# Keys, values and phi loaded as five tokens on partitions 0 to 63 and four on 64 to 127, with constant products from the first phi on

## The chip, the cores and the metric

The kernel runs on one core of a Trainium2 chip. The metric is the device time of one launch in microseconds (us). Three runs of the kernel before gave a median of 747.67 us (747.43 to 747.82). One more execution was taken by the profiler, and all rows below come from that one.

## What is computed

An attention with a memory of 32 slots per head, followed by a two-layer network with a squared ReLU:

```python
a = exp(phi - max(phi, axis=seq)); a = a / (sum(a, axis=seq) + 1e-9)    # phi: 8, 8, 576, 32
k_m = einsum("bhsm,bhsd->bhmd", a, k)                                    # q, k, v: 8, 8, 576, 64
v_m = einsum("bhsm,bhsd->bhmd", a, v)
attn = softmax(q @ k_m.T / 8)                                            # 576 x 32 per head
x = (attn @ v_m) as 4608 rows of 512
h = relu(x @ w_in)                                                       # 512 x 2048, float64
out = (h * h) @ w_out                                                    # 2048 x 512, float64
```

Sums over the sequence take tokens in any order, as long as phi, k and v have the same one.

## The kernel before

Everything is in float32, and the large products are made of pairs of reduced-precision parts (a high part `gh`, `ath`, `wi[.,0]` and a low part `glo`, `atl`, `wi[.,1]`), three products each. `w_in` and `w_out` come as float64 and are decoded on the chip (`decode`, L486): one 512 KB piece is loaded as `raw` (L501), taken apart by four VectorE instructions and one of ScalarE (L503 to L507), copied and subtracted (L516 to L528), and `w_in` is written back to a scratch in DRAM (`w_in_kept`, L530) for later rounds (`wi_again`, L534).

One unit of `memory(b, hh)` (L575) handles four heads of one batch: it loads phi, k and v, takes the largest phi (`fold` L568, `pmx` products L599 and L602, L601), subtracts it (L603), takes the exponential (L605), and forms sums (`pkv`, L633) and the products with k and v (`pkv`, `pkw`, L621). For the first two batches the products are scaled (L657, L658), turned (L656) and kept as `kbd` and as `VT` high and low (`values`, L712, L713, its high part by the helper of L418). There are 16 units. `attention(b)` (L969) loads q, forms scores (`psc`), a softmax (L960 to L966) and `ath`, `atl` (L945, L946); `mm1` and `mm2` (L1005, L1039) are the two layers for one slice of 128 of the 2048 hidden columns and one batch: `h` products at L1024, accumulations at L1055, L1056 and L1058. The last three batches take another path with fewer products (`fast`, L1136).

The tokens of a unit lie on the partitions as `tokens` (L543) puts them: 512 tokens as four on each of the 128 partitions, and the other 64 as a fifth on partitions 0 to 63, with two DMAs for each tensor. Partitions 64 to 127 have no fifth token; phi is filled with -3e38 there (L580). The products run over the five columns, the fifth with 64 partitions.

The order of all instructions is fixed by a planner when the program is built. Every operation is recorded with a cost for each engine that may do it, a set of things it reads and writes, and sometimes a due time. `order` (L169) makes keys from the latest possible start of each operation, adds 100 ns times an entry of the table `MOVED` by the operation's task number, and places the operations on the engines in a run through the plan (`forward`, L225); that order is then written out. DMAs are costed by their bytes and a rate by the size of one piece (`rate`, L420), and most are issued on SP's queue, in plan order; SP's queue waits at an instruction until its buffer is free, so all that stands behind it waits too. `filled` (L195) then walks over PE's operations and puts constant products (`filler`, L433: `minus` times `minus`, 128x512, into a PSUM bank that is free) into planned gaps. A gap is filled only between the planned times of `FILL`, from 18,000 ns on before; each product is taken for 230 ns, and before `WARM` (20,500 ns) only one product is written into a gap.

Of the kernel before, what the change touches and what calls it, by code (L numbers as in the profile page):

```python
# [19 lines left out]
P = 128  # L20
# [344 lines left out]
def tile_attention_moe(  # L365
# [177 lines left out]
    def tokens(d, dst, src):  # L543

        d(dst[:, :, 0:NMAIN], src[:, 0:SM].rearrange("h (p c) d -> p h c d", c=NMAIN))
        d(dst[0:LEFT, :, NMAIN], src[:, SM:S].rearrange("h p d -> p h d"))
# [942 lines left out]
```

## Time and profile before

| | before |
|---|---|
| median of 3 runs | 747.67 us |
| profiled execution | 747.32 us |
| its span | 745.6 us |
| instructions | 16009 |
| busy: PE / VectorE / ScalarE / GpSimd | 726.2 / 581.7 / 430.0 / 62.2 us |
| DMA packets, bytes | 82158, 136.22 MB |

The span runs from the first to the last instruction; the execution's own time has 1.7 us more around it. Busy time is the time that an engine's instructions cover. PE's rows are modelled at their ends, so a busy PE says that it did not wait, not that it ran at its best rate.

### The profile page before, as it was taken

Reading aid. Unit: us, or ns where it says so; the run is one execution under the profiler, and the core shown is the slowest. Engines: PE = TensorE matmul, PEld = TensorE weight load, DVE = VectorE, ACT = ScalarE, POOL = GpSimd, SP = SyncE. Lnnn points to the kernel's source line nnn. Section 1 sums busy time; section 2 is a strip of 40 time slices with the busy share of each in tenths; the row PEclk is TensorE's granted clock in tenths of the full one; section 3 lists DMA queues with packets and bytes.
Section 4 is the critical chain, followed back from the end, with each engine's and each line's share of the span. In section 5 each row is a group of like instructions: output and inputs, shape, how many; then the busy total and the mean of one; then the engine's idle time right before and its main releaser. Section 6 shows DMA issues by size and latency. Waiting matters only on the chain.

```text
span 745.6 us, 16009 instructions
## 1 busy us (share of the span) xinstructions
PE 726.2 (97%) x5879; PEld 640.0 (86%) x5879; DVE 581.7 (78%) x1513; ACT 430.0 (58%) x991; POOL 62.2 (8%) x119
## 2 busy tenths in 40 slices
PE   5999999999999999999999999999999999999997
PEld 4778888888878887888888788888999999999997
DVE  3899989975579779966554674999799768997984
ACT  2687789765553454644444433767477455665651
POOL 4100001000100100002121220001000010000000
PEclk9999999999999999999999999999999999999999
DMA  8988876674566756554899679103674255445521
GB/s 246 321 289 286 253 252 211 226 218 130 156 183 209 207 170 165 159 151 118 314 335 359 178 231 270 36 1 75 184 195 136 71 153 150 134 126 150 151 67 43
DMA packets 82158, 136.22 MB, mean 183 GB/s; under 512 B 26368, under 2 KB 52992, under 8 KB 82080
## 3 DMA queue, kind: packets, MB, share of 16 engines
q1 hardware_dynamic: 68704, 102.59, 47.5%
q0 software_dynamic: 13280, 32.48, 13.0%
q8 instruction: 47, 0.77, 0.4%
q14 instruction: 31, 0.25, 0.1%
q10 hardware_dynamic: 96, 0.13, 0.1%
HBM read 100.34 MB, written 34.80 MB: 181 GB/s over the span
## 4 chain that ended last, share of the span: by engine, by line
PE 80%; DVE 9%; DMA 6%; SPq 2%; issue 1%; ACT 1%; DVEq 0%; ACTq 0%
PE h L1024 14%; PE h L1162 10%; PE acc L1058 8%; PE acc L1055 8%; PE acc L1056 8%; PE accl L1274 3%; PE accl L1290 3%; PE pkv L621 3%; PE pvw L756 2%; DMA raw<-in_moe_w_out_dram 2%; PE pvq_pv L789 2%; DMA vw<-vw_kept 2%; PE psc L850 2%; PE Mb L1222 1%; PE Mb L1219 1%; PE Mc L1222 1%
## 5 line engine op out<-in xcount | busy, mean ns | idle before, releaser
L1024 PE MATMUL h<-ath,vw 128*128 128x256 f32 (+1 forms) x640 | 130.8, 301 | 0.0
L1055 PE MATMUL acc<-wo,gh 128*128 128x512 f32 x320 | 127.7, 399 | 0.0
L1056 PE MATMUL acc<-wo,gh 128*128 128x512 f32 x320 | 125.8, 393 | 0.0
L1024 PEld LDWEIGHTS h<-ath,vw 128*128 128x128 f32 x640 | 103.1, 189 | 9.7 <-issue 0.9
L1058 PE MATMUL acc<-wo,glo 128*128 128x512 f32 x320 | 110.1, 402 | 0.2 <-DVE glo L1034 0.2
L1162 PE MATMUL h<-ath,vw 128*128 128x256 f32 (+1 forms) x384 | 78.5, 297 | 2.8 <-DMA vw<-vw_kept 1.5
L1030 ACT ACTIVATE gh<-r 128x512 fp32r<-128x512 f32 x80 | 50.5, 633 | 50.9 <-PE acc L1056 42.6
L1034 DVE TENSOR_TENSOR glo<-r,gh 128x512 fp32r<-128x512 f32 x80 | 54.7, 686 | 23.1 <-PE acc L1058 12.3
L1058 PEld LDWEIGHTS acc<-wo,glo 128*128 128x128 f32 x320 | 58.8, 188 | 14.6 <-issue 1.3
L1055 PEld LDWEIGHTS acc<-wo,gh 128*128 128x128 f32 x320 | 60.3, 189 | 10.9 <-issue 0.8
L1056 PEld LDWEIGHTS acc<-wo,gh 128*128 128x128 f32 x320 | 60.3, 188 | 10.8
L1024 PE MATMUL h<-atl,vw 128*128 128x320 f32 (+1 forms) x320 | 68.7, 296 | 0.1
L1028 ACT ACTIVATE r<-h 128x320 f32<-128x320 f32 (+1 forms) x120 | 47.6, 408 | 28.4 <-PE h L1024 20.4
L1162 PEld LDWEIGHTS h<-ath,vw 128*128 128x128 f32 x384 | 59.6, 189 | 4.4 <-issue 2.4
L418 ACT CAST vw<-pvw 64x512 fp32r<-64x512 f32 (+1 forms) x64 | 37.2, 582 | 27.0 <-PE pvw L756 19.7
L1024 PEld LDWEIGHTS h<-atl,vw 128*128 128x128 f32 x320 | 51.4, 189 | 0.5 <-DVE atl L946 0.3
L1032 ACT ACTIVATE r<-r 128x576 f32<-128x576 f32 x68 | 46.5, 684 | 1.1
L1190 ACT CAST H<-X 128x512 fp32r<-128x512 f32 x48 | 29.7, 618 | 21.4 <-DVE X L1183 10.5
L1191 DVE TENSOR_TENSOR LA<-X,H 128x512 fp32r<-128x512 f32 x48 | 33.1, 690 | 10.3 <-ACT H L1190 9.4
L1162 PE MATMUL h<-atl,vw 128*128 128x256 f32 (+1 forms) x192 | 41.0, 295 | 0.0
L764 DVE TENSOR_TENSOR vw<-pvw,vw 64x512 fp32r<-64x512 f32 x48 | 33.0, 687 | 7.6 <-ACT vw L418 6.6
L1162 PEld LDWEIGHTS h<-atl,vw 128*128 128x128 f32 x192 | 30.8, 189 | 0.0
(238 smaller groups left out, 1745.9 us busy)
## 6 DMA issues: line engine op xcount, KB each, us to landing
vw<-vw_kept SPq DMA_DIRECT2D x224, 128.0 KB, 3.9
wi<-w_in_kept SPq DMA_DIRECT2D x40, 512.0 KB, 5.4
vw_kept<-fold POOLq DMA_DIRECT2D x32, 512.0 KB, 6.1
KV<-in_k_dram SPq DMA_DIRECT2D x16, 512.0 KB, 4.7
KV<-in_v_dram SPq DMA_DIRECT2D x16, 512.0 KB, 5.8
raw<-in_moe_w_out_dram SPq DMA_DIRECT2D x16, 512.0 KB, 4.6
raw<-in_moe_w_in_dram SPq DMA_DIRECT2D x16, 512.0 KB, 7.2
w_in_kept<-wi POOLq DMA_DIRECT2D x16, 512.0 KB, 4.4
```

The source lines that it names most:

```text
L418: nc.scalar.copy(o, i) if e == "ACT" else ENG[e].tensor_copy(o, i)
L764: vec({"DVE": 700}, lambda e, part=part, pr=pr: nc.vector.tensor_sub(part(1), pw()[pr], part(0).bitcast(F32)), [pw, (V, (0, hf))], [(V, (1 ...
L1024: nc.tensor.matmul(p()[:, 0:n], V()[:, l, hh, c0:c0 + P], x()[:, hh, cs], start=(i == 0), stop=(i == 5))
L1028: op({"ACT": act(n) - 40, **({} if b < 2 else {"DVE": tt(n)})}, lambda e, cs=cs, n=n, p=p: nc.scalar.activation(r()[:, cs], p()[:, 0:n], A ...
L1030: op({"ACT": act(SM)}, lambda e: nc.scalar.activation(gh(), r()[:, 0:SM], AF.Square), [r], [gh])
L1032: op({"ACT": act(S), **({} if b < 2 or b == FAST - 1 else {"DVE": tt(S)})}, lambda e: nc.scalar.activation(r(), r(), AF.Square) if e == "A ...
L1034: vec({"DVE": tt(SM)}, lambda e: nc.vector.tensor_sub(glo(), r()[:, 0:SM], gh().bitcast(F32)), [r, gh], [glo])
L1055: nc.tensor.matmul(a(), gh()[:, c], t()[:, 0], start=f0, stop=False)
L1056: nc.tensor.matmul(a(), gh()[:, c], t()[:, 1], start=False, stop=False)
L1058: nc.tensor.matmul(a(), glo()[:, c], t()[:, 0], start=False, stop=f1)
L1162: nc.tensor.matmul(p()[:, at:at + n], V()[:, l, hh, f0:f0 + P], x()[:, hh, cs], start=(i == 0), stop=(i == 5))
L1191: vec({"DVE": tt(w * P)}, lambda e, x=x, hi=hi, lo=lo: nc.vector.tensor_sub(lo().rearrange("p o f -> p (o f)"), x(), f32(hi())), src + [(H ...
```

## The change

The 576 tokens of a head are cut differently: 320 go as five to each of the partitions 0 to 63, and 256 as four to each of the partitions 64 to 127. Each tensor still takes two DMAs, now one for each half of the partitions. The computation on them stays as it was, since the fifth column still has 64 partitions. The planner's table of rates gets entries for the two new piece sizes. `FILL` starts at 2,600 ns, a product planned before `WARM` is taken for 460 ns, and a gap gets as many as fit, before `WARM` too. The table `MOVED` is another one, so that the order of most of the program is new.

```diff
--- before.py
+++ after.py
@@ -29,34 +29,33 @@
 LEAD = 9000
 PART = 12
 MOVED = {
-    3: -480, 10: -3, 11: -6, 12: -1857, 13: -293, 22: 16, 24: -61, 26: -179, 28: 907, 30: 489, 32: -418, 34: 108,
...
+    1: -1373, 2: -1775, 3: 343, 6: 5, 7: 2, 12: -569, 13: -129, 22: 34, 26: -1498, 28: 153, 38: -1375, 46: 1173,
...
 }
 SEES = {"DVE": 125, "ACT": 150, "PE": 200, "POOL": 60, "SP": 0}
 MARGIN = 250
 BANKS = "acc", "h", "pv", "pa"
-FILL = 18000, 90000
+FILL = 2600, 90000
 FREE = "h.0", "h.1", "pa.0", "pv.0", "acc.3", "acc.2", "acc.1", "acc.0"
 COLD, WARM = 1.8, 20500
 OPENS, SLOW, RAMP = 1950.0, 1.2, 7500
@@ -201,12 +200,13 @@
         holds, t, full = {}, FILL[0], []
         for o in out:
             if o.left == "PE":
-                n = int((o.start - t - 590) / 230)
+                each = 230 if t > WARM else 460
+                n = int((o.start - t - 590) / each)
                 idle = [x for x in FREE if x not in holds or (not left[holds[x][0]] and holds[x][1] + 300 < t)]
                 if n > 0 and idle and FILL[0] <= t < FILL[1]:
                     f = Op()
-                    f.ways, f.left, f.start, f.end = {"PE": 90 + 230 * n}, "PE", t, t + 90 + 230 * n
-                    f.fn, f.deps, f.users, f.lead = self.filler(idle[-1], n if t > WARM else 1), set(), [], True
+                    f.ways, f.left, f.start, f.end = {"PE": 90 + each * n}, "PE", t, t + 90 + each * n
+                    f.fn, f.deps, f.users, f.lead = self.filler(idle[-1], n), set(), [], True
                     full.append(f)
                 t = o.start + o.ways["PE"]
             for b in o.uses:
@@ -417,7 +417,7 @@
     def copy(e, o, i):
         nc.scalar.copy(o, i) if e == "ACT" else ENG[e].tensor_copy(o, i)
 
-    rate = {128: 100, 256: 220, 512: 288, 1024: 300, 2048: 312, 4096: 325, 4608: 190}
+    rate = {128: 100, 256: 220, 512: 288, 640: 292, 1024: 300, 1280: 303, 2048: 312, 4096: 325, 4608: 190}
 
     def dma(fn, parts, r=(), w=(), eng="SP", issue=520, **more):
 
@@ -542,8 +542,8 @@
 
     def tokens(d, dst, src):
 
-        d(dst[:, :, 0:NMAIN], src[:, 0:SM].rearrange("h (p c) d -> p h c d", c=NMAIN))
-        d(dst[0:LEFT, :, NMAIN], src[:, SM:S].rearrange("h p d -> p h d"))
+        d(dst[0:LEFT], src[:, 0:SC * LEFT].rearrange("h (p c) d -> p h c d", c=SC))
+        d(dst[LEFT:P, :, 0:NMAIN], src[:, SC * LEFT:S].rearrange("h (p c) d -> p h c d", c=NMAIN))
 
     def vt_alloc(n):
         for i in (0, 1) if n == 0 else (1 - n % 2,):
@@ -578,7 +578,7 @@
         A = st([P, 4 * SC * M], F32, "phi", f"phi{u}", 2)
         a = lambda: A().rearrange("p (h c m) -> p h c m", h=4, c=SC)
         op({"POOL": 200}, lambda e: nc.gpsimd.memset(a()[LEFT:P, :, NMAIN], -3e38), [], [(A, "pad")], lead=True)
-        dma(lambda d: tokens(d, a(), phi[b, 4 * hh:4 * hh + 4]), [(4 * SM * M * 4, 512), (4 * LEFT * M * 4, 128)], [], [(A, "in")], issue=600, lead=True)
+        dma(lambda d: tokens(d, a(), phi[b, 4 * hh:4 * hh + 4]), [(4 * SC * LEFT * M * 4, 640), (4 * (S - SC * LEFT) * M * 4, 512)], [], [(A, "in")], issue=600, lead=True)
         if where:
             KV = [(st([P, 4 * SC * D], F32, where[i], f"KV{u}_{i}"), None) for i in (0, 1)]
         else:
@@ -592,7 +592,7 @@
 
         for i, src in ((0, k), (1, v)):
             dma(lambda d, i=i, src=src: tokens(d, kv(i), src[b, 4 * hh:4 * hh + 4]),
-                [(4 * SM * D * 4, 1024), (4 * LEFT * D * 4, 256)], [], [KV[i]], issue=620, lead=True)
+                [(4 * SC * LEFT * D * 4, 1280), (4 * (S - SC * LEFT) * D * 4, 1024)], [], [KV[i]], issue=620, lead=True)
         mx = st([P, P], F32, "mx", f"mx{u}")
         fold(mx, A, a, nc.vector.tensor_max)
         pm = pt("pa", f"pmx{u}")
```

PE from its first instruction on (`idle` is the constant product, `pmx` the transposes for the largest phi, `pkv` and `pkw` the unit's sums and products, `pq` the turned q). Before:

```order
L599 MATMUL pmx_0_117<-ident,mx_0_105 128x128
L602 MATMUL pmx_0_117<-ident,mc_0_119 128x128
L599 MATMUL pmx_1_136<-ident,mx_1_124 128x128
L633 MATMUL pkv_0_140<-ones,phi_0_83 32x1 x20
L602 MATMUL pmx_1_136<-ident,mc_1_138 128x128
L621 MATMUL pkv_0_140<-KV_0_97,phi_0_83 32x64 x20
L621 MATMUL pkw_0_190<-KV_0_97,phi_0_83 32x64 x20
L633 MATMUL pkv_1_217<-ones,phi_1_87 32x1 x20
```

and now:

```order
L440 MATMUL idle<-minus 128x512 x5
L599 MATMUL pmx_0_123<-ident,mx_0_105 128x128
L602 MATMUL pmx_0_123<-ident,mc_0_125 128x128
L440 MATMUL idle<-minus 128x512 x3
L633 MATMUL pkv_0_141<-ones,phi_0_83 32x1 x20
L621 MATMUL pkw_0_164<-KV_0_93,phi_0_83 32x64 x20
L621 MATMUL pkv_0_141<-KV_0_93,phi_0_83 32x64 x20
L599 MATMUL pmx_1_220<-ident,mx_1_185 128x128
L888 MATMUL pq_0_0_227<-ident,q_0_108 128x128 x4
```

Eight constant products stand ahead of the first sums, and the second unit's `pmx` went behind the first unit's products.

VectorE in the stretch of the first attention's softmax (`S`, `red`, `rz`, L960 to L966), with the phi of the second batch's first unit (`mc`, `phi`) and decode rows (`work`) between. Before:

```order
L965 RECIPROCAL rz_1_450<-rz_1_450 128x20
L505 TENSOR_SCALAR work<-raw 128x512
L966 TENSOR_TENSOR S_1_412<-S_1_412,rz_1_450 128x640
L946 TENSOR_TENSOR atl_481<-pat_0_453,ath_460 128x512
L503 TENSOR_SCALAR work<-raw 128x512
L506 SCALAR_TENSOR_TENSOR work<-raw,work 128x512
L505 TENSOR_SCALAR work<-raw 128x512
L946 TENSOR_TENSOR atl_481<-pat_1_487,ath_460 128x512
L507 SCALAR_TENSOR_TENSOR work<-work 128x512
L953 TENSOR_TENSOR atl_481<-patl_493,ath_460 128x2x64
L503 TENSOR_SCALAR work<-raw 128x512
L601 TENSOR_REDUCE mc_0_523<-pmx_0_483 128x1
```

and now:

```order
L601 TENSOR_REDUCE mc_0_454<-pmx_0_450 128x1
L961 TENSOR_TENSOR S_1_434<-S_1_434,red_1_448 128x640
L965 RECIPROCAL rz_0_436<-rz_0_436 128x16
L505 TENSOR_SCALAR work<-raw 128x512
L966 TENSOR_TENSOR S_0_390<-S_0_390,rz_0_436 128x512
L603 TENSOR_TENSOR phi_0_225<-phi_0_225,pmx_0_450 128x640
L963 TENSOR_REDUCE rz_1_476<-S_1_434 128x20
L505 TENSOR_SCALAR work<-raw 128x512
L964 TENSOR_SCALAR rz_1_476<-rz_1_476 128x20
L503 TENSOR_SCALAR work<-raw 128x512
L965 RECIPROCAL rz_1_476<-rz_1_476 128x20
L946 TENSOR_TENSOR atl_501<-pat_0_471,ath_489 128x512
```

The reduce of `pmx` (L601) and the subtraction from phi (L603) of that unit, which stood behind the second `atl` row before, stand ahead of the first one now, and one more piece's decode (the second L505 row) has begun ahead of it.

SP's queue where pieces of w_in are read again for the second batch (`wi`, L536), with `raw` pieces and q of the third batch (L832) between. Before:

```order
L501 DMA raw<-in_moe_w_in_dram 128x2x512
L536 DMA wi_0_1_1143<-w_in_kept 128x1024
L501 DMA raw<-in_moe_w_out_dram 128x1024
L832 DMA q_1_1201<-in_q_dram 64x1152
L536 DMA wi_1_0_1212<-w_in_kept 128x1024
L536 DMA wi_1_1_1214<-w_in_kept 128x1024
L832 DMA q_1_1201<-in_q_dram 64x1152
```

and now:

```order
L536 DMA wi_0_0_1057<-w_in_kept 128x1024
L501 DMA raw<-in_moe_w_out_dram 128x1024
L536 DMA wi_0_1_1166<-w_in_kept 128x1024
L501 DMA raw<-in_moe_w_out_dram 128x1024
L536 DMA wi_1_0_1182<-w_in_kept 128x1024
L536 DMA wi_1_1_1249<-w_in_kept 128x1024
L832 DMA q_1_1256<-in_q_dram 64x1152 x2
L536 DMA wi_2_0_1277<-w_in_kept 128x1024
```

The pieces `wi_1_0` and `wi_1_1` went ahead of both loads of q, of which one stood ahead of them before.

## Rows read from the trace of the kernel before

**Rows 1.** The page, busy time of each engine (share of the span) and instructions.

```profile
PE 726.2 (97%) x5879; PEld 640.0 (86%) x5879; DVE 581.7 (78%) x1513; ACT 430.0 (58%) x991; POOL 62.2 (8%) x119
```

**Rows 2.** Table by stretch: from:to, length, busy of each engine, granted clock, DMA.

```profile
core 0: us, PE busy (x) PEld busy (x) DVE busy (x) ACT busy (x) POOL busy (x), PEclk, DMA share, GB/s
0.00:3.00 3.00, 0.00 (x0) 0.00 (x0) 0.06 (x1) 1.59 (x2) 2.13 (x13) 1.00 0.27 69
3.00:5.00 2.00, 0.00 (x0) 0.00 (x0) 1.12 (x3) 0.00 (x0) 2.00 (x2) 1.00 0.76 189
5.00:10.00 5.00, 2.53 (x45) 1.45 (x45) 3.03 (x12) 0.74 (x1) 3.70 (x4) 1.00 0.94 246
10.00:15.00 5.00, 4.90 (x127) 3.94 (x126) 1.93 (x6) 0.91 (x2) 0.20 (x1) 1.00 1.11 293
15.00:18.00 3.00, 2.77 (x52) 1.92 (x50) 1.04 (x5) 0.85 (x4) 0.00 (x0) 1.00 1.10 360
40.00:90.00 50.00, 50.00 (x528) 42.70 (x527) 47.25 (x115) 39.78 (x85) 4.70 (x10) 1.00 0.84 273
157.50:161.60 4.10, 4.10 (x24) 3.51 (x23) 1.53 (x4) 1.18 (x3) 0.00 (x0) 1.00 1.02 251
212.30:217.70 5.40, 5.40 (x36) 4.91 (x35) 5.30 (x10) 4.34 (x10) 0.00 (x0) 1.00 1.00 230
```

**Rows 3.** Chain of waits: start us, length us, what; 0 to 100 us.

```profile
11.88 9.20 DMA raw<-in_moe_w_out_dram
...
37.94 1.66 PE h L1024 x9
39.60 0.86 PE pd L521 x2
40.46 0.23 PE pd L522
40.69 0.11 PE pmx L602
...
43.95 0.53 PE pkv L633 x40
...
84.94 8.91 DMA wi<-w_in_kept
```

**Rows 4.** VectorE in order of time: start us, us, line, operation, idle before.

```profile
15.11 0.36 DVE L418 CAST VTh<-pvt 128x64 fp32r<-128x64 f32 x2 [0.94 <-PE pvt L656]
...
16.97 0.35 DVE L657 TENSOR_SCALAR kvx<-pkv,rs 128x128 f32<-128x128 f32 x1 [1.17 <-PE pkv L621]
21.10 0.43 DVE L505 TENSOR_SCALAR work<-raw 128x512 uint32<-128x512 uint32 x1 [3.78 <-DMA raw<-in_moe_w_out_dram]
21.44 0.42 DVE L503 TENSOR_SCALAR work<-raw 128x512 f32<-128x512 f32 x1
...
22.64 0.68 DVE L507 SCALAR_TENSOR_TENSOR work<-work 128x512 uint32<-128x512 uint32 x1
...
30.04 0.82 DVE L960 TENSOR_REDUCE red<-S 128x20 f32<-128x640 f32 x1 [0.70 <-ACT S L930]
...
38.93 0.29 DVE L601 TENSOR_REDUCE mc<-pmx 128x1 f32<-128x128 f32 x1
...
41.61 0.83 DVE L603 TENSOR_TENSOR phi<-phi,pmx 128x640 f32<-128x640 f32 x1
```

**Rows 5.** PE in order of time, same columns.

```profile
20.66 3.52 PE L913 MATMUL psc<-kbd,qT 128*128 128x64 f32 x16
...
27.25 1.97 PE L913 MATMUL psc<-kbd,qT 128*128 128x64 f32 x16
...
90.91 0.71 PE L736 MATMUL pvw<-wi,VTh 128*128 128x256 f32 x4 [0.41 <-DMA wi<-w_in_kept]
...
93.89 0.74 PE L736 MATMUL pvw<-wi,VTh 128*128 128x256 f32 x4 [1.34 <-DMA wi<-w_in_kept]
```

**Rows 6.** SP's DMA issues in order of time, same columns, around 211 us.

```profile
210.98 2.41 SPq L832 DMA_DIRECT2D q<-in_q_dram  x4
```

43 rows, old and new, of the table MOVED are left out of this document.

## Prediction

> **What bounds the kernel now.** I read the busy times first, then the table by stretch, then the chain of waits, and then each engine's rows at the places the chain names. TensorE is busy for 726.2 us of a span of 745.6 [rows 1], so about 19 us are lost, and from 40 to 90 us it is busy for 50.00 of 50.00 [rows 2]. The loss sits at the start: no PE work in the first 5 us, 2.53 of 5 in the next [rows 2]. From about 37 us on PE is full, so a change to the start is worth exactly what it does to the moment when PE becomes full, less the real work that PE has done by then.
>
> What sets that moment? The chain goes back from the first `h` product at 37.94 through VectorE's rows to one transfer: the first piece of w_out, issued at 11.88, which takes 9.20 us [rows 3]. VectorE waits 3.78 us for it and starts decoding at 21.10 [rows 4]; from there to 37.9 it has a single pause that matters, 0.70 us before the reduce at 30.04 [rows 4]. So up to 21.1 the start is bound by the transfers in SP's queue (DMA share 0.94, 1.11, 1.10 from 5 us on [rows 2]), and after it by VectorE. TensorE is not what the start waits for, though its rows there are slow: the 16 `psc` matmuls took 3.52 us at 20.66 and 1.97 at 27.25 [rows 5]. The table prints a granted clock of 1.00 from the first stretch on [rows 2], but the same shape at 1.8 times the time can only be the lower level, 1.2 GHz, and the later one 2.4.
>
> A comparison at 0.2%, 1.5 us, is about what a measurement of this kernel can tell from no change. The sum below is made against the profiled execution, 747.32 us; the median of the runs, 747.67, lies 0.35 above it, and I add that at the end.
>
> **Part 1: the loads.** Ahead of the w_out piece the queue carries two units of phi, K and V, and two q loads, before and after alike. One unit is 4 heads x 576 tokens x (32 + 64 + 64) x 4 bytes = 1.475 MB, two are 2.95 MB. Before, they moved mostly between 5 and 15 us at 246 and 293 GB/s [rows 2], mean 270, so 10.9 us. The change keeps the bytes and the number of DMAs, makes the pieces longer (phi 512 and 128 bytes become 640 and 512, keys and values 1024 and 256 become 1280 and 1024) and fewer (768 per load become 512), but each DMA now fills only 64 partitions. The kernel has such a transfer already: a q load (L832) fills 64 partitions with 4608 bytes each, and they come in pairs, lower half, upper half. Four of them issued at 210.98 [rows 6] fill the stretch from 212.3 to 217.7, and there the queues are busy all the time (share 1.00) at 230 GB/s; in a stretch where one q load shares the queue with a 512 KB load of w_in it is 251 at a share of 1.02 [rows 2]. The loads over all 128 partitions reached 293 and 360 [rows 2]. So halves are slower per byte although their pieces are the largest in the program.
>
> The price: at 230 the 2.95 MB take 12.8 us, +1.9; at 251, 11.8 us, +0.8; at 360, which is the other bound, 8.2 us, -2.7. I take 251, because at the start halves stand between 128-partition loads (q, w_out) as in that row. The Trainium skill, SBUF — State Buffer, section "Door 1: The DMA port swizzle", says that DMA bandwidth follows the number of the 16 ports that the partitions reach and that 64 consecutive partitions reach half of them; with half of its 435 GB/s my estimate from that page is 13.6 us, +2.7, and the whole sum below would be +1.6 and not -0.3. The 230 of the q loads agrees with that rule nearly in full.
>
> Against this stands a gap that the first loads leave: DMA share 0.27 in the first 3 us and 0.76 in the next two [rows 2], when SP had issued 0.59 MB of phi, with 32 KB pieces between. Now the second load is a value load, and the first four DMAs carry 0.88 MB. At most 0.5 us (0.24 x 2) from 3 to 5 and as much around it can be won: 0 to -1.0, I take -0.5. The w_out piece lands **+0.3 us** (bounds -3.7 and +1.9).
>
> **Part 2: VectorE's work ahead of the first `h`.** The new order puts eight more VectorE instructions between the first decode row and the second `atl` subtraction, on which `h` waits (37 instructions before, 45 now): one each of L503, L505, L507, L657, L601 and L603 and two L418. By their rows that is 0.42 + 0.43 + 0.68 + 0.35 + 0.29 + 0.83 and 0.36 for the two, together 3.4 us; but rows that follow each other start sooner than they end (21.10, then 21.44 for one of 0.43 [rows 4]), about 0.08 each, so **+2.7 us** (bounds 2.0, if some fill the pause, and 3.4). None of it is new work: it is taken out of the time behind 40 us, but there VectorE is not what PE waits for (PE 50.00 of 50.00 while VectorE has 47.25 [rows 2]), so nothing comes back for it directly.
>
> What does come back is PE's own work: ahead of the first `h` the new order has one `pmx` transpose, 40 `pkv` sums and the `pd` pair of the first w_out piece, which stood behind it before. At the warm price of the chain that is 0.11 + 0.53 + 0.86 + 0.23 = **-1.7 us** [rows 3].
>
> **Part 3: the constant products.** Eight of them now stand ahead of the first sums, in gaps where PE waits for phi, and four more later in ones and twos; they use `minus` and a free PSUM bank, and hold nothing up as long as phi's chain leaves PE idle for the first 5 us [rows 2]. If PE rises to 2.4 GHz with them, `psc` at 3.52 could take 1.97, but the work that waits for it is in VectorE's queue behind three decodes, and those wait for the transfer. All that a warm clock can give is the pause of 0.70 us [rows 4]: 0 to -0.7, I take **-0.4**.
>
> **Part 4: the order behind the start.** At 84.94 the chain waits 8.91 us for a load of w_in [rows 3], and PE stands 0.41 us at 90.91 and 1.34 at 93.89 for it [rows 5]: 1.75 us, the largest stop of PE behind the start. In that place SP now issues both w_in pieces ahead of the two q loads of the next attention; before, one q load stood in front. That is 288 KB less ahead of them, at 230 GB/s 1.3 us. I take **-1.2** (0, if the queue behind it is slower, to -1.75). MOVED reorders everything else too; those places I do not price, take 0, and leave 1.5 us to both sides.
>
> **The sum:** +0.3 + 2.7 - 1.7 - 0.4 - 1.2 = -0.3 us, 747.0 us for a profiled execution and **747.4 us** as a median: no change that could be told. Its own range is 746.2 to 749.1.
>
> **Rival A, faster: the halves cost nothing.** If fewer and longer pieces count and the halves overlap (one DMA engine in the lower half while another is already in the upper), the loads run between 293 and 360, say 327 GB/s [rows 2]: 9.0 us, -1.9, and with the gap -2.4 for the w_out piece. The rest of the sum with the whole 1.75: -2.4 + 2.7 - 1.7 - 0.4 - 1.75 = -3.55, about **744.1 us**. For it: the longer pieces, a queue that never empties from 5 us on. Against it: the 230 and 251 GB/s of the only halves in the trace.
>
> **Rival B, slower: the halves share a limit.** Mechanism: two DMAs of one load follow each other on the same queue, both engines' shares go to the same 64 partitions, and each load moves at the q loads' 230 GB/s; the early gap is then eaten too. The w_out piece lands 1.9 later, VectorE's 2.7 come on top, PE's 1.7 go off, no clock gain, and the w_in loads at 90 us come behind slower key and value loads, so that stop stays: 1.9 + 2.7 - 1.7 = +2.9, **750.6 us**. It decides when the stretch from 5 to 18 us falls under some 250 GB/s. The page named in part 1 speaks for this rival; the trace's q loads too.
>
> **Rival C, the change does not do what it says:** the clock stays at the lower level until about 27 us in spite of the products, because PE rests between them. Then only the 0.4 of part 3 go, 747.8 us; it lies within the forecast.
>
> **Chances.** Forecast (with C) 0.43, A 0.30, B 0.27. The forecast is likeliest because the bounds of part 1 have different signs and the pieces of the other parts nearly cancel. A is over 0.2% faster, B over 0.2% slower, the forecast within it, so the three chances are these. To leave out 2 in 10 in all, the range has to reach to the middle of both rivals: 744.0 to 751.0.
>
> **What will show it.** In the table by stretch, GB/s between 5 and 15 us: about 250 for the forecast, 230 or less for B, over 300 for A. In VectorE's rows, the start of the first decode: 21.4; 23.0 for B; 18.7 for A. The first `h` product of PE: 40 us, with fewer constant products just ahead of it than the four of before. `psc` near 2 us instead of 3.52 if the clock rises early. No stop of over 0.5 us for w_in near 90 us. The prediction is wrong in its core if PE's first full stretch begins at a time that the landing of the first w_out piece does not explain, or if the time moves by over 2 us through stops behind 100 us.

## The result, and the profile after

The changed kernel takes **752.5 us** (median of 4 runs, 752.06 to 752.73), the kernel before 747.55 in runs beside them (747.35 to 747.82): a ratio of 1.0065, 95% interval 1.0048 to 1.0083. It is 5 us slower. The forecast was 747.4 with a range up to 751.0, so the prediction was wrong, in sign and in range; the rival that ended slower gave 750.6. The profiled execution took 752.73 us with a span of 750.9.

The page of the changed kernel, busy time of each engine, against [rows 1]:

```profile
PE 729.1 (97%) x5882; PEld 643.4 (86%) x5882; DVE 582.8 (78%) x1513; ACT 430.8 (57%) x991; POOL 62.6 (8%) x119
```

Then the table by stretch of the changed kernel, same columns as [rows 2] (the last three: granted clock, DMA share, GB/s):

```profile
0.00:3.00 3.00, 0.53 (x1) 0.50 (x2) 0.06 (x1) 1.59 (x2) 2.08 (x13) 1.00 0.15 39
3.00:5.00 2.00, 1.97 (x5) 0.99 (x3) 0.32 (x2) 0.00 (x0) 2.00 (x2) 1.00 0.81 197
5.00:10.00 5.00, 3.12 (x53) 1.99 (x57) 2.44 (x6) 0.74 (x1) 3.79 (x4) 1.00 1.10 227
10.00:15.00 5.00, 3.13 (x82) 2.13 (x78) 1.81 (x8) 0.00 (x0) 0.15 (x1) 1.00 1.14 227
15.00:18.00 3.00, 2.93 (x13) 2.51 (x12) 1.45 (x5) 1.53 (x4) 0.05 (x1) 1.00 1.11 237
20.00:30.00 10.00, 7.39 (x69) 6.47 (x69) 6.50 (x16) 3.71 (x7) 0.20 (x1) 0.56 1.11 279
30.00:40.00 10.00, 9.74 (x37) 6.37 (x35) 5.88 (x17) 4.69 (x11) 1.48 (x3) 0.59 1.10 261
```

and the last two of these stretches in the kernel before:

```profile
20.00:30.00 10.00, 9.85 (x56) 8.83 (x56) 8.08 (x17) 6.74 (x17) 0.39 (x2) 1.00 1.12 297
30.00:40.00 10.00, 9.31 (x50) 6.56 (x48) 9.96 (x27) 6.75 (x15) 1.69 (x4) 1.00 1.05 366
```

Three things are to be seen. From 5 to 18 us the queues are no less busy than before (share 1.10 to 1.14) and move 227, 227 and 237 GB/s where before they moved 246, 293 and 360 [rows 2]. From 20 to 40 us VectorE, which was to be full, is busy for 12.38 of 20 us (6.50 + 5.88); before it was 18.04. And the granted clock is 0.56 and 0.59 there, so PE spends most of that time at 1.2 GHz; in the kernel before, it stayed up once it had risen.

VectorE of the changed kernel in order of time (start us, us, operation, idle before in brackets), to be held against [rows 4]:

```profile
23.08 0.43 DVE L505 TENSOR_SCALAR work<-raw 128x512 uint32<-128x512 uint32 x1 [3.80 <-DMA raw<-in_moe_w_out_dram]
...
24.36 0.34 DVE L658 SCALAR_TENSOR_TENSOR kvx<-pkw,rs,par 128x128 f32<-128x128 f32 x1
...
25.56 0.34 DVE L657 TENSOR_SCALAR kvx<-pkv,rs 128x128 f32<-128x128 f32 x1
...
27.52 0.43 DVE L505 TENSOR_SCALAR work<-raw 128x512 uint32<-128x512 uint32 x1 [0.42 <-DMA raw<-in_moe_w_in_dram]
...
30.29 0.69 DVE L960 TENSOR_REDUCE red<-S 128x16 f32<-128x512 f32 x1 [0.20 <-ACT S L918]
...
35.91 0.82 DVE L960 TENSOR_REDUCE red<-S 128x20 f32<-128x640 f32 x1 [2.35 <-ACT S L930]
...
38.24 0.29 DVE L601 TENSOR_REDUCE mc<-pmx 128x1 f32<-128x128 f32 x1 [1.43 <-PE pmx L599]
```

And its PE, against [rows 5]:

```profile
20.41 0.96 PE L621 MATMUL pkv<-KV,phi 128*32 128x64 f32 x40 [0.72 <-DMA KV<-in_k_dram]
21.32 1.97 PE L888 MATMUL pq<-ident,q 128*128 128x128 f32 x8
24.76 0.48 PE L656 MATMUL pvt<-ident,kvx 128*128 128x128 f32 x1 [1.48 <-DVE kvx L658]
25.96 3.67 PE L913 MATMUL psc<-kbd,qT 128*128 128x64 f32 x16 [0.72 <-DVE kvx L657]
...
31.28 3.64 PE L913 MATMUL psc<-kbd,qT 128*128 128x64 f32 x16
...
46.06 0.40 PE L1024 MATMUL h<-ath,vw 128*128 128x256 f32 x2
...
86.02 0.73 PE L1058 MATMUL acc<-wo,glo 128*128 128x512 f32 x2 [0.93 <-DVE glo L1034]
...
522.51 0.28 PE L1219 MATMUL Ma<-wo,H 128*128 128x256 f32 x1
```

The first w_out piece is there 1.98 us later (23.08 against 21.10). The products for `kvx` of the second unit end near 21.4 on PE, but the two VectorE rows that take them (24.36, 25.56) stand behind the first decode, which waits for that piece. PE has `pvt` and both `psc` queued behind `kvx`, so the first `psc` comes at 25.96 instead of 20.66. (In the kernel before, one of the two rows, L657 at 16.97 [rows 4], was done ahead of the decode; the other, L658 at 22.38, came behind its start as well, but there PE had the first `psc` in front of `pvt`.) The second one, at 1.2 GHz, then keeps VectorE waiting for 2.35 us, and `pmx` behind it for 1.43. The first `h` product is 8.8 us late (46.06 against 37.29). Not all of that is lost: the last stage of the program, marked by its first product into Ma, starts 4.5 us late, against this row of the kernel before:

```profile
518.02 0.28 PE L1219 MATMUL Ma<-wo,H 128*128 128x256 f32 x1
```

### The profile page after: what moved, and what is told of

The parts are those of the page before. It is cut to its first block, busy times and chain, and to the rows that moved or that the text cites. A ratio compares the mean times of both kernels' runs of the same rounds, so it can differ in the third digit from the quotient of the medians.

```text
span 750.9 us, 16024 instructions
## 1 busy us (share of the span) xinstructions
PE 729.1 (97%) x5882; PEld 643.4 (86%) x5882; DVE 582.8 (78%) x1513; ACT 430.8 (57%) x991; POOL 62.6 (8%) x119
## 4 chain that ended last, share of the span: by engine, by line
PE 86%; DMA 6%; issue 3%; DVE 2%; SPq 1%; ACT 0%; POOL 0%; DVEq 0%; POOLq 0%
PE h L1024 16%; PE h L1162 10%; PE acc L1058 9%; PE acc L1055 9%; PE acc L1056 9%; PE accl L1290 3%; PE accl L1274 3%; PE pkv L621 2%; PE pvw L756 2%; PE pvq_pv L789 2%; PE psc L850 2%; DMA vw<-vw_kept 2%; PE Ma L1222 2%; PE Ma L1219 1%; PE Ma L1220 1%
## 5 line engine op out<-in xcount | busy, mean ns | idle before, releaser
L1024 PE MATMUL h<-ath,vw 128*128 128x320 f32 (+1 forms) x640 | 130.0, 300 | 0.1
L1058 PE MATMUL acc<-wo,glo 128*128 128x512 f32 x320 | 107.2, 402 | 0.9 <-DVE glo L1034 0.9
L1162 PE MATMUL h<-ath,vw 128*128 128x256 f32 (+1 forms) x384 | 79.8, 297 | 3.4 <-DMA vw<-vw_kept 3.0
L1024 PE MATMUL h<-atl,vw 128*128 128x256 f32 (+1 forms) x320 | 68.5, 295 | 0.0
L1024 PEld LDWEIGHTS h<-atl,vw 128*128 128x128 f32 x320 | 51.5, 189 | 0.1
L1162 PE MATMUL h<-atl,vw 128*128 128x256 f32 (+1 forms) x192 | 41.0, 295 | 0.0
L1029 DVE TENSOR_SCALAR r<-h 128x320 f32<-128x320 f32 (+1 forms) x41 | 18.6, 457 | 19.2 <-PE h L1024 18.5
```

The lines of the kernel that those rows point to most:

```text
L1024: nc.tensor.matmul(p()[:, 0:n], V()[:, l, hh, c0:c0 + P], x()[:, hh, cs], start=(i == 0), stop=(i == 5))
L1058: nc.tensor.matmul(a(), glo()[:, c], t()[:, 0], start=False, stop=f1)
L1162: nc.tensor.matmul(p()[:, at:at + n], V()[:, l, hh, f0:f0 + P], x()[:, hh, cs], start=(i == 0), stop=(i == 5))
```

## The experiments

One table serves them all: when (us) the first decode of VectorE, the two `psc`, the first `h` and the first Ma product start in each kernel's profile, and the ratio of its time to the kernel before, run beside it. In these runs the executions of one kernel spread wider than in the first ones (the kernel before: 742.6 to 752.5 in one set), so the intervals are wide, and one profile is one execution; I read mechanisms from the rows and verdicts from the ratios.

| kernel | decode | psc | psc | h | Ma | ratio, 95% interval |
|---|---|---|---|---|---|---|
| before | 21.10 | 20.66 | 27.25 | 37.29 | 518.02 | 1 |
| changed | 23.08 | 25.96 | 31.28 | 46.06 | 522.51 | 1.0065 (1.0048 to 1.0083) |
| changed, once more | 23.12 | 25.99 | 31.31 | 46.09 | 522.36 | 1.0075 (1.0032 to 1.0119) |
| before, new loads | 23.25 | 23.19 | 29.84 | 39.93 | 520.55 | 1.0052 (1.0028 to 1.0076) |
| before, early products | 20.09 | 20.00 | 25.14 | 36.59 | 516.32 | 1.0005 (0.9987 to 1.0023) |
| changed, no early products | 23.04 | 25.91 | 31.23 | 46.03 | 521.40 | 1.0074 (1.0047 to 1.0100) |
| changed, old loads | 20.81 | 23.77 | 28.68 | 43.73 | 519.72 | 1.0046 (1.0013 to 1.0078) |
| changed, kvx first | 22.71 | 22.84 | 29.93 | 44.73 | 520.15 | 1.0035 (1.0017 to 1.0052) |
| changed, 15 products more | 22.62 | 29.70 | 32.85 | 44.47 | 519.84 | 1.0092 (1.0062 to 1.0122) |
| changed, halves on two queues | 22.26 | 25.39 | 29.00 | 42.76 | 520.35 | 1.0046 (1.0028 to 1.0064) |
| changed, kvx first, old loads | 20.55 | 20.34 | 26.58 | 41.38 | 516.63 | 0.9992 (0.9962 to 1.0022) |
| the same, whole unit first | 19.39 | 19.23 | 21.97 | 38.79 | 514.00 | 1.0003 (0.9988 to 1.0018) |
| before, early and late products | 19.73 | 18.73 | 24.77 | 37.72 | 517.11 | 0.9994 (0.9967 to 1.0021) |
| before, loads cut by heads | 21.58 | 21.06 | 27.71 | 37.75 | 515.80 | one execution, 749.38 us |
| before, loads cut by partitions | 24.25 | 23.77 | 30.43 | 41.37 | 520.20 | one execution, 750.61 us |

**The three parts of the change, one at a time.** First the kernel before with the new loads alone:

```diff
-        d(dst[:, :, 0:NMAIN], src[:, 0:SM].rearrange("h (p c) d -> p h c d", c=NMAIN))
-        d(dst[0:LEFT, :, NMAIN], src[:, SM:S].rearrange("h p d -> p h d"))
+        d(dst[0:LEFT], src[:, 0:SC * LEFT].rearrange("h (p c) d -> p h c d", c=SC))
+        d(dst[LEFT:P, :, 0:NMAIN], src[:, SC * LEFT:S].rearrange("h (p c) d -> p h c d", c=NMAIN))
```

> The kernel before with nothing changed but the two loads of each tensor (halves of the partitions); order and constant products stay as before. Load theory (the slow halves are what costs): the first w_out piece lands 2 us later, near 23.1, VectorE's first decode starts there, and the time rises by 2 to 5 us, to 749.5 to 752.5. Clock theory (the early constant products let the clock rise too early, and it falls back in the next hole): no early products, so PE rises once, near 27 to 30 us, and does not fall; at most the 2.0 us of the later piece, 749.5. Order theory (the new table is what costs): the same 749.5 or less, since the old order hides some of it.

Measured: 1.0052, decode at 23.25. The load theory holds: with order and products untouched, the halves alone cost 0.28 to 0.76%, 2.1 to 5.7 us.

The reverse, the changed kernel with these four lines turned back:

> The changed kernel with the loads of before (all partitions with four tokens, then the left ones); order, rates in the plan and constant products as in the change. Load theory: the w_out piece lands near 21.1, and the time comes back to 747 to 748.5. Clock theory: the early products are still there; if the clock falls again the time is 750 to 751, if the earlier piece closes the holes at 22 to 26 us it does not fall, and the time is 746 to 748. Order theory: 750 or more in spite of the old loads, with first h behind 41 us.

Measured: decode at 20.81, yet 1.0046 and the first `h` at 43.73. So the loads are not the whole; the new order costs something even where w_out is early. The interval overlaps that of the changed kernel, so what the old loads give back in this order is read from the rows alone.

The early products alone, in the old order, and the new order without them:

```diff
-FILL = 18000, 90000
+FILL = 2600, 90000
...
-                n = int((o.start - t - 590) / 230)
+                each = 230 if t > WARM else 460
+                n = int((o.start - t - 590) / each)
...
```

> The kernel before with nothing changed but the rule for constant products (from 2.6 us on; it puts six and two of them ahead of the first sums). Clock theory: if early products alone do the harm, the granted clock rises near 17 us and is back at 0.50 for some stretch behind 20 us, and the time is 750 or more; if they do harm only together with holes in PE's row, nothing falls here, since PE has no hole of 0.5 us between 15 and 33 us in this order: psc takes 1.97 at both places and the time is 746.9 to 747.6. Load and order theories: no difference, 747.3 to 747.8.

> The changed kernel with the old rule for constant products (none before 18 us). Clock theory: the granted clock rises once, between 26 and 30 us, and no stretch shows 0.50 behind it; psc at 31 us takes about 2 instead of 3.64 and the first pd pair 1.1 instead of 2.08, so the first h product comes 3 to 5 us earlier than at 46.06 and the time is 748 to 750. Load theory: the w_out piece still lands near 23.1 and the time stays within 1 us of 752.5. Order theory: also 752.5.

Measured: no difference that can be told in either order (1.0005; 1.0074 beside 1.0065 and 1.0075). In the old order the products did what part 3 had hoped for, `psc` near 2 us at both places:

```profile
20.00 1.94 PE L914 MATMUL psc<-kbd,qT 128*128 128x64 f32 x16
...
25.14 2.03 PE L914 MATMUL psc<-kbd,qT 128*128 128x64 f32 x16 [1.62 <-ACT kbd L670]
```

but the times don't show it (that the first `h` comes 0.70 us earlier there is no sign of it either, since w_out landed 1.01 us earlier in that execution). In the new order the first `h` is at 46.03 without them and 46.06 with them. That they were what made the clock fall is refuted: without them it fell as well (the second unit's `pkw` took 0.90 us at 17.75, and `psc` 3.67 at 25.91).

**The changed kernel once more**, as the measure for the next three:

> The changed kernel itself once more, as the measure for the three runs beside it. Its ratio to the kernel before should again be near 1.0065 (about 752 where before has 747). All theories agree on that; what differs is the clock: where the granted clock rises and falls in the first 45 us may differ between executions, and each such difference should move the first h product by no more than 2 us.

Measured: 1.0075, every landmark within 0.2 us. In this execution the rows show no early rise of the clock at all (the second unit's `pkw` took 1.45 us at 18.68, in the first profile 0.90 at 18.79), and the first `h` is in the same place (46.09). The short rise moved nothing in these rows.

**What holds psc.** The rows that make `kvx` go ahead of the decode on VectorE; the order is re-sorted after the plan, and only the decode rows and what depends on them move:

```diff
+        last = [o for o in out if "kvx" in names(o)][3]
...
+            if t < last.start and ("tf" in names(o) or "W" in names(o)):
+                t = last.start + 1
```

> The changed kernel, with the two rows that make kvx of the second unit (L658, L657) ahead of the first decode on VectorE instead of among its rows, where they wait for w_out although their inputs are there near 21 us. Queue theory (VectorE's wait for w_out holds kvx, kvx holds pvt and psc on PE): the first psc starts near 23.5 instead of 25.96, PE has no stop of over 0.5 us between 22 and 26 us, the first h product comes 2 to 3 us earlier, near 43.5, and the time falls by 1.5 to 3 us. Load theory: w_out still lands near 23, VectorE stays the bound behind it, and the time changes by less than 0.7 us. Clock theory: only if the granted clock does not fall to 0.50 in this run does the time change, then by 3 us or more.

Measured: 1.0035 where the changed kernel has 1.0075, with intervals that overlap, so the gain in time is not clear by this run alone; the first `psc` at 22.84, as the queue theory said. The first `h` gained 1.4 us only, since the second `psc` now stood 2.96 us for ScalarE's copy to `kbd`.

**Holding the clock** with 15 products more, ahead of four operations of PE counted in its order:

```diff
-        holds, t, full = {}, FILL[0], []
+        holds, t, full, more = {}, FILL[0], [], iter([{4: 4, 13: 2, 16: 6, 17: 3}.get(i, 0) for i in range(9999)])
...
-                n = int((o.start - t - 590) / each)
+                n = max(int((o.start - t - 590) / each), next(more))
```

> The changed kernel with 15 more constant products in PE's holes (four ahead of the first pkv, two ahead of the second unit's pkv, six ahead of its pvt, three ahead of the first psc). Clock theory: PE does not rest between 9 and 26 us, the granted clock rises before 21 us and no stretch behind shows 0.50; both psc take about 2.0 instead of 3.67 and 3.64, the first pd pair 1.1 instead of 2.08; the first h product comes 3 to 5 us earlier and the time falls by 2 to 4 us. Load and queue theories: what PE waits for is VectorE, so the rows of PE are shorter but the first h product moves by under 1.5 us and the time by under 1 us.

Measured: the two `psc` take 2.00 and 1.97, the granted clock is 1.00 from 30 to 40 us, and the first `h` comes 1.6 us earlier. The time does not fall: 1.0092. The test isn't a clean one, for the six products themselves came to stand 2.69 us behind `kvx`. It shows no more than that two warm `psc` and an earlier first `h` did not bring the time back here; the next run has both `psc` warm too (1.96 and 1.97), its first `h` 3.3 us earlier than the changed kernel's, and 1.0046.

**Why a half is slow.** First the upper halves of the first batch's keys and values on ScalarE's queue, beside the lower ones:

```diff
-            dma(lambda d, i=i, src=src: tokens(d, kv(i), src[b, 4 * hh:4 * hh + 4]),
+            dma(lambda d, i=i, src=src: tokens(d, kv(i), src[b, 4 * hh:4 * hh + 4], nc.scalar.dma_start if b == 0 else None),
...
-        d(dst[LEFT:P, :, 0:NMAIN], src[:, SC * LEFT:S].rearrange("h (p c) d -> p h c d", c=NMAIN))
+        (d2 or d)(dst[LEFT:P, :, 0:NMAIN], src[:, SC * LEFT:S].rearrange("h (p c) d -> p h c d", c=NMAIN))
```

> The changed kernel with the upper halves of the first batch's keys and values issued from ScalarE's queue, so that they move beside the lower halves and not behind them; bytes and pieces are the same. If a half is slow because it fills only 64 partitions, the two kinds together move faster: over 270 GB/s between 5 and 15 us instead of 227, the w_out piece lands at 20 to 21.5 instead of 23.1, and the time falls by 1.5 to 3 us. If the longer pieces themselves or the order of the loads are what is slow: still about 227 GB/s, 23 us and no change in the time beyond 1 us.

Measured: between the two, 245 GB/s from 5 to 15 us, decode at 22.26, 1.0046. Then the pair that leaves pieces, bytes and the number of DMAs alike, and cuts the old four-token load once by heads (the first two new lines) and once by partitions (the last three), each in place of the first line:

```diff
-        d(dst[:, :, 0:NMAIN], src[:, 0:SM].rearrange("h (p c) d -> p h c d", c=NMAIN))
+        d(dst[:, 0:2, 0:NMAIN], src[0:2, 0:SM].rearrange("h (p c) d -> p h c d", c=NMAIN))
+        d(dst[:, 2:4, 0:NMAIN], src[2:4, 0:SM].rearrange("h (p c) d -> p h c d", c=NMAIN))
...
+        main = src[:, 0:SM].rearrange("h (p c) d -> p h c d", c=NMAIN)
+        d(dst[0:LEFT, :, 0:NMAIN], main[0:LEFT])
+        d(dst[LEFT:P, :, 0:NMAIN], main[LEFT:P])
```

> The kernel before with each load of the four tokens (128 partitions, four heads) cut in two by heads: two DMAs of two heads each over all 128 partitions, then the left tokens; 1024-byte pieces as before, three DMAs a tensor instead of two. It is the measure for the run beside it. Between 5 and 15 us the rate stays near the 270 GB/s of before, if the number of DMAs does not bound it; if SP's issuing (0.65 us each, six more) bounds it, the rate falls below 250 and the DMA share below 0.9.

> The kernel before with the same load cut in two by partitions: 0 to 63, then 64 to 127, four heads each; number of DMAs, bytes and pieces (1024 bytes) exactly as in the run that cuts by heads. If a DMA that fills only 64 partitions is what is slow: 220 to 240 GB/s between 5 and 15 us, 30 GB/s or more under the cut by heads, at a share of 1.1, and the w_out piece lands 1 to 2 us later than there. If instead the longer pieces (1280 bytes) or the order of the loads made the change's loads slow: the two cuts agree within 10 GB/s and 0.5 us.

Table by stretch, cut by heads:

```profile
5.00:10.00 5.00, 2.45 (x44) 1.45 (x44) 3.03 (x12) 0.74 (x1) 3.78 (x4) 1.00 0.78 231
10.00:15.00 5.00, 4.34 (x125) 3.50 (x125) 2.00 (x6) 0.74 (x1) 0.20 (x1) 1.00 0.98 277
15.00:18.00 3.00, 2.84 (x46) 1.93 (x46) 0.81 (x5) 1.00 (x3) 0.00 (x0) 1.00 1.11 333
```

and cut by partitions:

```profile
5.00:10.00 5.00, 1.84 (x35) 1.02 (x35) 3.90 (x11) 0.74 (x1) 3.70 (x4) 1.00 0.90 196
10.00:15.00 5.00, 4.30 (x141) 3.25 (x133) 1.84 (x5) 0.74 (x1) 0.20 (x1) 1.00 1.14 244
15.00:18.00 3.00, 2.23 (x38) 1.83 (x38) 1.00 (x6) 1.00 (x3) 0.00 (x0) 1.00 1.15 213
```

The cut by partitions keeps the queues busier and moves less, 35 GB/s less in the first and 33 in the middle stretch, and its decode starts 2.67 us later. The last stretch is no fair pair: by 18 us the cut by heads had moved about 4.09 MB and the other 3.26 (227 and 181 GB/s over 18 us), so it was already at another load. Three more DMAs a unit cost something as well: from 5 to 15 us the cut by heads moves 254 GB/s at a share of 0.88, the kernel before 270 at 1.03. These are single executions; how far such can differ is seen from the kernel before and the two with early products in the old order, whose loads are the same and whose first decode starts at 21.10, 20.09 and 19.73. The 2.67 us is nearly twice the spread of those three. With pieces of the same size in both, it is by this pair the 64 partitions that make a half slow; whether the longer pieces or the order of the loads add to it was not tried.

**Both costs taken out together**, old loads and `kvx` first, in the new order:

> The changed kernel's order and constant products with both suspected costs taken out: kvx of the second unit ahead of the first decode on VectorE, and the loads of before. If load and queue together are what the change costs: the w_out piece lands near 21, psc starts near 22, the last stage's first accumulation (Ma, L1219), at 518.0 us in the kernel before and 522.5 in the changed one, comes at 517 to 518.5, and the time is within 0.2% of before. If the rest of the new order costs something of its own (order theory): the last stage still starts 2 us or more late, 520 or later, and the time is 1.003 or more of before.

Measured: 0.9992 (0.9962 to 1.0022), Ma at 516.63. The interval lies clear of the changed kernel's, 1.0032 at the least. Load and queue together account for the loss; the rest of the new order costs nothing that can be told. How the loss divides between them is not settled by the times: each run with one of the two taken out overlaps this one and the changed kernel.

VectorE of this kernel still has 2.95 us of pauses on the way to its first `h`:

```profile
31.22 0.82 DVE L969 TENSOR_REDUCE red<-S 128x20 f32<-128x640 f32 x1 [1.52 <-ACT S L939]
...
33.55 0.29 DVE L610 TENSOR_REDUCE mc<-pmx 128x1 f32<-128x128 f32 x1 [1.43 <-PE pmx L608]
```

and that `h` comes at 41.38, 4.1 us later than before, at the same time of the whole. PE still stops too, and the clock falls:

```profile
20.34 1.90 PE L922 MATMUL psc<-kbd,qT 128*128 128x64 f32 x16
...
23.90 0.44 PE L907 MATMUL pql<-ident,qx 128*128 128x128 f32 x2 [1.54 <-ACT qT L900]
...
26.58 3.65 PE L922 MATMUL psc<-kbd,qT 128*128 128x64 f32 x16 [1.78 <-ACT kbd L678]
```

So the last kernel moves the second unit's copies on ScalarE and its `pkt` on PE ahead of the decode as well (the same re-sorting, for ScalarE's decode rows and the first `psc`; the constant products ahead of that `pkt` are left out):

```diff
+            if t < kbd.start and (decode(o, "ACT") or has(o, "ACT", "flat")):
+                t = kbd.start + 1
+            if o is psc:
+                t = max(t, max(x.start for x in turned) + 1)
```

> The changed kernel's order with the loads of before, and with the second unit's whole chain ahead of the first decode: its kvx on VectorE, its two copies to kbd and the second half of qT on ScalarE, its pkt ahead of the first psc on PE. With kvx alone moved, PE still stood 1.54 us before pql and 1.78 us before the second psc, which took 3.65 us because the granted clock had fallen at 24.8. If what the second psc waited for is ScalarE's queue, both stops go, the second psc starts near 23 instead of 26.58 and takes 2.0, the last stage starts 1 to 2.5 us earlier than 516.6, and the time is 0.995 to 0.999 of before. If VectorE's decode is the bound there whatever PE does: the second psc is earlier but the first h product stays near 41.4, and the time stays within 0.1% of the run with kvx alone moved (0.9992 of before).

```profile
19.23 1.90 PE L931 MATMUL psc<-kbd,qT 128*128 128x64 f32 x16
...
21.97 1.97 PE L931 MATMUL psc<-kbd,qT 128*128 128x64 f32 x16
27.35 0.70 PE L944 MATMUL pscl<-kbd,qx 128*64 128x64 f32 x8 [3.41 <-ACT qx L919]
```

ScalarE's queue it was: both stops are gone, the second `psc` is at 21.97 and the first `h` at 38.79. But the edit put a stop of 3.41 us behind it, where ScalarE's copy to `qx` now waits behind its own decode rows, and the time is that of before, 1.0003. The profiled execution was the fastest of twelve (744.15, median 747.15), so its Ma at 514.00 can't be carried over to the time. No kernel here beats the one before.

**The spread.** Last, the kernel before with the early products and eight more at the start of the last stage (ahead of its four stops):

```diff
+        more = {fast[2]: 1, fast[3]: 1, fast[6]: 4, next(o for o in out if o.fn.__name__ == "mm7"): 2}
...
+                n = max(int((o.start - t - 590) / each), more.get(o, 0))
```

> The kernel before with the early constant products and with eight more at the start of the last stage (one ahead of the third and of the fourth h there, two ahead of the first Mb, four ahead of the seventh h, which waits for a load of vw). It asks where the spread between executions (744 to 752) comes from. If it is a fall of the granted clock after the stops at 513 to 523 us in some executions: no fall there any more, a median of 745 to 746.5 and a spread of under 3 us. If the spread comes from the start: no change, 747, spread as before, within 0.1% of the kernel with the early products alone.

Measured: the stops from 520 to 530 us are closed (PE 10.00 of 10.00 busy), the median is 746.56, and nine of the ten executions lie between 745.4 and 747.9; the tenth took 751.3. So these stops are not the whole of the spread.

That they are a part of it is seen in other profiles. The seventh `h` of the last stage waits for a load of `vw`, here in the kernel before and in the changed kernel with old loads, whose profiled execution (755.67) was 5.5 us over the median of its ten:

```profile
523.07 0.47 PE L1162 MATMUL h<-ath,vw 128*128 128x256 f32 x2 [0.98 <-DMA vw<-vw_kept]
526.91 0.77 PE L1162 MATMUL h<-ath,vw 128*128 128x256 f32 x2 [3.96 <-DMA vw<-vw_kept]
```

From the first Ma to the end of the span the second of these takes 233.9 us, and its granted clock is 0.67 from 524 to 530 us. Two more profiles show a clock under 1.00 near there (the cut by heads, with a stop of 2.73 us, and the changed kernel without early products, 2.12), and they take 231.6 and 230.4; all others take 227.6 to 229.1, with stops of up to 2.30. What made the execution of 751.3 long has no trace and stays open.

## Why the prediction was wrong

**What bounds the kernel** was right in the place: the time was lost at the start, and from 100 to 500 us PE is busy for 398.25 us, before 398.94 (eight stretches of 50 us of the table, added up). "TensorE is not what the start waits for" no longer held in the new order, and the prediction's own sign of being wrong came: the landing of w_out (+1.98) does not explain when the first `h` starts (+8.8).

**Part 1 was mis-sized.** "I take 251", +0.3 us: measured are 227, 227 and 237 GB/s and +1.98, the upper bound (+1.9) that the prediction had from the four q loads at 230 [rows 6]. The row of 251 was a mean over a half and a full load, and here the halves come twelve in a row, with only q between. The gap that was to give back 0.5 gave nothing: 39 and 197 GB/s from 0 to 5 us, 69 and 189 before [rows 2]. The Trainium skill, SBUF — State Buffer, section "Door 1: The DMA port swizzle", says that 64 consecutive partitions reach half of the 16 ports, and would have given +2.7 for the same load by my estimate from it. The pair cut by heads and by partitions agrees with that in kind, and the measured +1.98 decides the size. Two queues side by side reached 245 GB/s, so overlap gave a part of it back, no more.

**Part 2 failed, and it is the step that cost the sign.** The +2.7 us for eight more VectorE rows took for granted that VectorE would run without a pause from its first decode on, as it had in [rows 4]. From that decode to the first `h` it took 22.98 us (23.08 to 46.06) where before it took 16.19: +6.8. First the kernel before, then the changed one:

```profile
21.10:37.29 16.19, 15.48 (x85) 12.31 (x85) 15.32 (x37) 11.32 (x25) 1.92 (x4) 1.00 1.09 327
23.08:46.06 22.98, 19.36 (x121) 14.36 (x121) 18.44 (x45) 13.19 (x27) 2.04 (x4) 0.67 1.10 285
```

VectorE was busy for 18.44 us against 15.32, so the eight rows cost 3.1, near the 2.7. The other 3.7 are idle time, for which the sum had nothing: pauses of 0.42, 0.20, 2.35 and 1.43 us, 4.40 together, where before it had one of 0.70. I counted how many rows stood ahead of `h`, but did not ask which rows had gone behind the wait for w_out: the two that make the second unit's `kvx`. The runs with `kvx` moved show that this order holds the first `psc` back (25.96 to 22.84) and that, with the old loads, the loss goes away with it. They do not show that every pause costs time: with both taken out 2.95 us of pauses and 4.1 us of a late first `h` are left, and the time is that of before. How much of the 3.7 was paid for is open.

The whole difference of the two spans, +5.3 us, is +1.98 to the first decode, +6.79 from there to the first `h`, -4.28 from there to the first Ma, and +0.81 behind it. The sum had +0.3, +2.3 (2.7 less the 0.4 of part 3), -2.9 (1.7 and 1.2) and nothing. What came back between the first `h` and the first Ma is read from these stretches, before and changed:

```profile
37.29:518.02 480.73, 476.33 (x3668) 400.86 (x3667) 372.26 (x890) 284.97 (x628) 47.31 (x89) 1.00 0.65 200
46.06:522.51 476.45, 473.11 (x3625) 400.67 (x3623) 372.10 (x885) 282.65 (x623) 46.82 (x88) 1.00 0.68 198
```

PE is busy there for 3.22 us less (1.7 of it is the work that part 2 named as done earlier; the rest was not traced) and idle for 1.06 less. So the terms that give back were right in sign, and 1.4 us too small together; the load and the pauses outweighed them.

**Part 3** took 0.4 us off; the early products change nothing that can be measured. Its reason, "the work that waits for it is in VectorE's queue behind three decodes", holds for the old order; in the new one VectorE's pause of 2.35 us ends with ScalarE's copy out of `pscl`, which PE does right behind its second `psc` of 3.64 us. That the clock could fall again and stay low until 38 us, later than before, no rival had.

**Part 4** was right: no stop of PE for w_in near 90 us is left (0.41 and 1.34 before [rows 5]); one of 0.93 for `glo` stands in its neighbourhood.

**The rivals.** B had the mechanism and the place of the load (first decode at 23.0 forecast, 23.08 measured; under 250 GB/s), and gave 750.6. It missed the queue behind that wait, and it kept the stop near 90 us, which went. A is refuted by the rate. C, "the clock stays at the lower level", gave 747.8, because a cold `psc` was thought to be covered; it was not.

In sum: old loads alone bring Ma from 522.5 to 519.7, `kvx` alone to 520.15, both to 516.6 (5.9 us, where the two add up to 5.2), as far as single profiles tell: with the order of before and loads that are not halved, Ma lies between 515.8 and 518.0 in four of them.

## What to carry to other kernels

When a planner's order changes, look at the wait that bounds the start, and list for each engine what now stands behind it although its inputs are ready; counting rows ahead of a milestone is not enough. Nor is a late milestone lost time as such: here a first `h` 4.1 us late cost nothing, since the way from it to the first Ma was 5.5 us shorter. A load that fills only 64 partitions is priced from a row of such loads alone, not from a mixed one: here it was 2 us on 21. Constant products made `psc` nearly twice as fast in places, and the times of no kernel showed it.

## What was not expected of the hardware

From 15 to 18 us the kernel with its loads cut by partitions moved 213 GB/s at a DMA share of 1.15, the one cut by heads 333 at 1.11, with in part another load: a busy share over 1.1 does not tell how many bytes move.

The granted clock of the changed kernel fell near 21 us, in the middle of PE's work:

```profile
18.00:19.00 1.00, 0.74 (x56) 0.72 (x59) 0.46 (x4) 0.79 (x2) 0.00 (x0) 1.00 1.10 228
19.00:20.00 1.00, 0.69 (x40) 0.43 (x28) 0.25 (x2) 0.00 (x0) 0.00 (x0) 1.00 1.12 311
20.00:21.00 1.00, 0.59 (x33) 0.53 (x33) 0.00 (x0) 0.00 (x0) 0.00 (x0) 1.00 1.04 404
21.00:22.00 1.00, 1.00 (x17) 0.83 (x12) 0.00 (x0) 0.00 (x0) 0.20 (x1) 0.56 1.10 308
```

Its largest stop in the three us before was 0.72 us; the stops of 1.48 and 0.72 us ahead of `pvt` and `psc` came after the fall. In the kernel before, with PE busy for 9.85 us from 20 to 30, the clock rose between its two `psc` (3.52 us at 20.66, 1.97 at 27.25 [rows 5]) and stayed up. Two executions of one kernel differed in whether the clock rose before 20 us, and their first `h` still came within 0.03 us.
